# Ending a unit's output products as P6, P3, P7, P7, P3 in other PSUM banks, and rounding the turns on ScalarE: a fused gated linear attention and ELU MLP

## The chip, the core and the metric

The kernel runs on one core of a Trainium2 chip. Five engines share the work: PE (TensorE, matmuls; PEld is its weight load), DVE (VectorE), ACT (ScalarE), POOL (GpSimd) and SP (SyncE, which issues most of the DMAs). The metric is the device time of one execution in microseconds (us); smaller is better.

## What is computed

```
for t in range(S):                       # q, k, v, a_re, a_im: B=4, H=8, S=768, D=48
    new_re = ar * S_re - ai * S_im       # a scaled to a magnitude of at most 0.999
    new_im = ar * S_im + ai * S_re
    S_re, S_im = new_re + k_t v_t^T, new_im
    y[t] = q_t @ S_re
x = y as (B*S, H*D)                      # 3072 tokens x 384
h = x @ w_in                             # 384 x 2048, float64 in memory
g = where(h > 0, h, exp(min(h, 0)) - 1)  # ELU
out = g @ w_out                          # 2048 x 384, float64 in memory
```

## The kernel before

The 3072 tokens are worked off in 12 units, u = 0 to 11, of two batches times 128 tokens. For each unit the attention part gives x, the first MLP product gives h, ELU gives g, and the second product gives the rows of the output. The recurrence is solved in chunks: decays are summed up within a chunk by matmuls (`turned` at L847 for the phases), gates are made from exponentials and sines, and a state `S` is carried from unit to unit.

Units 0 and 1 run plainly while the weights arrive and `convert` turns their float64 words into float32 on DVE. From unit 3 on, h comes from 20 smaller products per unit (`mult`, L1505, eight matmuls each), whose sums are put together by DVE and ACT: `joint` (L1521) adds two of them, `low` (L1526 and L1527, ACT) makes the exponential of ELU, `whole_of` (L1530, DVE) finishes a block of g. `mixed` and `mixed_rest` (L1465, L1485) make the sums of x from which those products start.

From unit 2 on, the second product is also made of seven smaller ones, P1 to P7, each in two halves h = 0 and 1 of eight matmuls (`product`, L1369). Some take sums of blocks of g, which `folded` (L1347, DVE) makes. The results lie in three PSUM tiles of two places each, named (bank, place) here: the tile of bank 0 holds P1, P2 and P3 one after the other at place 0 and P6 at place 1; that of bank 1 holds P5 at place 0 and P7 at place 1; that of bank 2 holds P4. At P6's end DVE adds P6 to a copy of P1 (L1381, into `u2`) and P5 to that (L1382, into `u4`). P7's, P2's and P3's ends (`done`, L1394) write the output rows: three DVE operations for P7, one for P3, a copy on ACT for P2.

`turned` takes the turns of the phase from PSUM, rounds them to a whole number on DVE by adding and subtracting a large constant (L852), and subtracts that from the turns, again on DVE (L855). `waves` then takes sines of it on ACT (L983 to L987), behind a load of ACT's table. `decayed`, `slopes` and `used` are the exponentials of the decays (L914, L930). `scaled` (L1002 for q on DVE, L992 for k on POOL) and `gated` (L1013, q on DVE and k on POOL) make the operands that PE transposes (L1033). `state_sums` (L1089 on DVE, with L1091 on POOL between two of them) adds up the new state; `seam` (L1240) hands x over by DMA; L1260 are the plain MLP products of the units 0 to 2.

Each engine works through its instructions strictly in the order in which the program emits them, and waits at semaphores for other engines. That order is set by hand. For the start and the units 0 to 2 there is a list, `first`. All behind it comes from `plan`: each step is put at a planned time inside its unit, plus a number from the table `SHIFT` (with `@u`, for unit u alone), and the steps are emitted in the order of these times. In the units 10 and 11 the last products run as P6, P6, P3, P7, P7, P3 (each name one half), in the others as P6, P6, P7, P7, P3, P3.

Of the kernel before, what the change touches and what calls it, by code (L numbers as in the profile page):

```python
# [13 lines left out]
ALU = mybir.AluOpType  # L14
# [491 lines left out]
def kernel(  # L506
# [63 lines left out]
    ln_eps = value(float(np.log(2 * EPS)), "ln_eps")  # L570
    quarter = value(float(np.pi / 2), "quarter")
# [270 lines left out]
    def turned(u, n):  # L842
        x = nat[u]
        if n == 0:
# [7 lines left out]
        nc.vector.tensor_scalar(  # L852
            out=z, in0=t, scalar1=MAGIC, scalar2=MAGIC, op0=ALU.add, op1=ALU.subtract
        )
        nc.vector.tensor_tensor(out=z, in0=t, in1=z, op=ALU.subtract)  # L855
# [389 lines left out]
    def hidden(u, f):  # L1245
        inner(u, f)
        elu(u, f)
# [101 lines left out]
    def product(u, k, h):  # L1349
# [3 lines left out]
            1: (0, 0, True), 2: (0, 0, False), 6: (0, 1, False), 5: (1, 0, True),  # L1353
            7: (1, 1, False), 3: (0, 0, True), 4: (2, 0, True),
# [25 lines left out]
        if k == 6:  # L1380
            nc.vector.tensor_tensor(out=u2, in0=to, in1=u2, op=ALU.add)  # L1381
            nc.vector.tensor_tensor(out=u4, in0=x["p", 1][:, 0], in1=u2, op=ALU.add)  # L1382
            return
# [219 lines left out]
    def warm(n):  # L1603
# [23 lines left out]
        "transposed('q', 1)@5": -0.2, "used()": 0.5, "waves()": 0.8, "waves()@3": -3.0,  # L1627
        "whole_of('00', '00')@11": -0.1, "whole_of('00', '00')@3": 0.8,
        "whole_of('10', '10')@4": 0.2, "whole_of('11', 'w')": 0.05, "whole_of('11', 'w')@3": 0.05,
        "whole_of('21', '21')": 0.05, "whole_of('21', '21')@3": 0.05, "whole_of('21', '21')@4": 0.3,  # L1630
        "whole_of('21', '21')@5": 0.1,
# [27 lines left out]
    def gates_of(u, *at):  # L1659
# [8 lines left out]
        (squared, "ai", 1), (joined, 0, 1), (joined, 0, 0), (logarithms, 0, 1), (logarithms, 0, 0),  # L1668
        (ratios, 0, 0), (lengths, 0, 1), (lengths, 0, 0), (sums, 1), (powers, 0, 1), (powers, 0, 0),
        (sums, 0), (warm, 2), (ratios, 0, 1), *2 * [(convert,)], (table, "trig_and_small", 0),  # L1670
# [3 lines left out]
        (scaled, 0, "k", 0), (begun, 1), (ends, 0), (table, "natural_log_exp_and_others", 0),  # L1674
        (scaled, 0, "q", 0), (warm, 2), (warm, 1), (gated, 0, 0), (warm, 1), (scaled, 0, "q", 1),
        (scaled, 0, "k", 1), (warm, 1), (squares, 1), (transposed, 0, "q", 0), (gated, 0, 1),
        (warm, 1), (transposed, 0, "k", 0), (convert,), (joined, 1), (transposed, 0, "q", 1),
        (convert,), (scores, 0, 0), *2 * [(convert,)], (load_qk, 1), (logarithms, 1), (powers, 1),
        (transposed, 0, "k", 1), (lengths, 1), (states, 0, 0), (convert,), (ratios, 1), (warm, 2),
        (slopes, 1), (noted, 1), (values, 0, 0), (convert,), (decays, 1), (warm, 2), (scores, 0, 1),  # L1680
        (states, 0, 1), (angles, 1), (load_v, 1), (warm, 2), (values, 0, 1), (seam, 0), (noted, 0),
        (carry_on, 0), (fetch, "in", 3), (convert,), (scaled, 1), (warm, 2), (ends, 1),
# [44 lines left out]
    def layer_of(u, at_h, at_p):  # L1727
# [33 lines left out]
        if u > NU - 3:  # L1761
            ks[-4:] = (3, 0), (7, 0), (7, 1), (3, 1)
# [105 lines left out]
```

## Time and profile before

| | |
|---|---|
| median of three runs | 648.45 us (648.39, 648.45, 649.2) |
| the profiled execution | 648.65 us, of which the span is 646.9 |
| PE busy | 632.3 us, 98% of the span |
| DVE, ACT, POOL busy | 506.3, 416.8, 168.2 us |
| granted TensorE clock | 0.99 of full speed over the span |

The span is what the profiler sees from the first instruction to the last. A row of the timeline reads: start in us, duration in us, engine, line, operation, output and inputs with their shapes, how many alike were put together, and in brackets how long the engine stood idle before and what released it. A unit is 49 us long in the middle of the run; the first unit's MLP products begin at 44.84 us, and the last matmul ends at 640.7.

### The profile page before, as it was taken

How to read it: one execution, taken by the hardware profiler on the slowest of the kernel's cores; microseconds unless marked ns; L12 is line 12 of the kernel's file. 1: busy time of each engine (PE TensorE's matmuls, PEld its weight loads, DVE VectorE, ACT ScalarE, POOL GpSimd, SP SyncE). 2: the span in 40 equal slices, each digit the busy share in tenths (PEclk: the TensorE clock that was granted, in tenths of full speed). 3: DMA queues.
4: the chain of work that ended last, by engine and by line, in shares of the span. 5: the costliest groups of instructions: out<-in, count | busy, mean ns of one | idle time of the engine just before them, and what ended most of it. 6: DMA issues, size and time to landing. Idle time of an engine off the chain costs nothing.

```text
span 646.9 us, 17126 instructions
## 1 busy us (share of the span) xinstructions
PE 632.3 (98%) x7236; PEld 577.6 (89%) x7236; DVE 506.3 (78%) x801; ACT 416.8 (64%) x684; POOL 168.2 (26%) x200
## 2 busy tenths in 40 slices
PE   8999999999999999999999999999999999999995
PEld 5878886677899999999999999999998999999995
DVE  6999999969689798689589589589679678675481
ACT  5985573765867767776776776766775776661350
POOL 2010100113125415414514513613613603502000
PEclk9889999999999999999999999999999999999999
DMA  9988559435600824424335334344343342112100
GB/s 164 175 138 142 132 164 197 113 67 79 94 9 16 141 51 96 103 57 96 87 61 108 75 70 108 73 76 97 75 84 86 73 97 63 39 31 62 35 2 30
DMA packets 150705, 56.10 MB, mean 87 GB/s; under 512 B 128948, under 2 KB 142428, under 8 KB 150620
## 3 DMA queue, kind: packets, MB, share of 16 engines
q1 hardware_dynamic: 146880, 53.57, 41.3%
q0 software_dynamic: 3520, 1.20, 1.6%
q8 instruction: 59, 0.97, 0.6%
q14 instruction: 26, 0.21, 0.1%
q10 hardware_dynamic: 220, 0.14, 0.1%
HBM read 48.91 MB, written 4.80 MB: 83 GB/s over the span
## 4 chain that ended last, share of the span: by engine, by line
PE 91%; SPq 4%; DVE 2%; DMA 1%; issue 1%; ACT 1%; DVEq 0%; ACTq 0%
PE mlp L1369 29%; PE mlp L1505 16%; PE mlp L1260 10%; PE y L1505 8%; PE w L1033 6%; PE w L1074 4%; PE y L1285 3%; PE mlp L1285 3%; PE y L1119 3%; PE y L1189 3%; PE w L847 2%; PE y L1110 2%; SPq L654 2%; SPq L603 1%; DMA w<-in_moe_w_in_dram 1%; PE w L899 1%
## 5 line engine op out<-in xcount | busy, mean ns | idle before, releaser
L1369 PE MATMUL mlp<-w_out,g 128*128 128x192 f32 x640 | 111.8, 328 | 1.0 <-DVE ee L1381 1.0
L1369 PEld LDWEIGHTS mlp<-w_out,g 128*128 128x128 f32 x640 | 104.2, 190 | 4.4 <-DVE ee L1381 1.6
L1091 POOL TENSOR_TENSOR S<-S,T 128x384 f32<-128x384 f32 x36 | 32.4, 899 | 198.1 <-DVE S L1089 198.1
L1260 PE MATMUL mlp<-x,w_in 128*128 128x256 f32 x288 | 64.0, 381 | 0.0
L1521 DVE TENSOR_TENSOR g<-g,mlp 128x512 f32<-128x512 f32 x45 | 30.9, 686 | 42.2 <-ACT qt L1034 25.3
L1260 PEld LDWEIGHTS mlp<-x,w_in 128*128 128x128 f32 x288 | 54.6, 191 | 7.8
L1347 DVE TENSOR_TENSOR g<-g 128x512 f32<-128x512 f32 x80 | 54.4, 702 | 4.6 <-PE mlp L1369 3.6
L1505 PE MATMUL mlp<-x,w_in 128*128 128x128 f32 x424 | 56.1, 276 | 0.0
L1369 PE MATMUL mlp<-w,g 128*128 128x192 f32 x320 | 54.5, 329 | 0.0
L1240 POOL DMA_DIRECT2D x<-y x62 | 30.7, 502 | 85.8 <-ACT y L1136 54.2
L1369 PEld LDWEIGHTS mlp<-w,g 128*128 128x128 f32 x320 | 51.8, 190 | 0.6
L1526 ACT ACTIVATE ee<-g 128x512 f32<-128x512 f32 x63 | 39.5, 626 | 19.7 <-DVE g L1521 18.5
L1505 PEld LDWEIGHTS mlp<-x,w_in 128*128 128x128 f32 x424 | 51.6, 192 | 0.1
L1530 DVE SCALAR_TENSOR_TENSOR g<-ee,g 128x512 f32<-128x512 f32 x63 | 43.9, 697 | 5.8 <-ACT ee L1527 5.5
L1527 ACT ACTIVATE ee<-ee 128x512 f32<-128x512 f32 x72 | 45.4, 631 | 2.3
L1518 ACT COPY g<-mlp 128x512 f32<-128x512 f32 x36 | 20.9, 582 | 36.0 <-PE mlp L1505 36.0
L1227 ACT COPY x<-y 128x384 f32<-128x384 f32 x20 | 8.6, 482 | 38.1 <-PE y L1119 38.1
L1034 ACT COPY qt<-w 128x512 f32<-128x512 f32 x48 | 25.6, 592 | 11.3 <-PE w L1033 11.3
L914 ACT ACTIVATE n<-w 64x384 f32<-64x384 f32 (+1 forms) x60 | 28.1, 486 | 4.8 <-PE w L899 4.0
L1250 ACT ACT_TABLE_LOAD x24 | 30.8, 1283 | 0.5
L1089 DVE TENSOR_TENSOR S<-w,S 128x384 f32<-128x384 f32 x38 | 21.1, 555 | 11.5 <-PE w L1074 5.3
L1505 PE MATMUL mlp<-x,g 128*128 128x128 f32 x224 | 29.6, 275 | 0.0
(226 smaller groups left out, 1447.5 us busy)
## 6 DMA issues: line engine op xcount, KB each, us to landing
w<-in_moe_w_out_dram SPq DMA_DIRECT2D x8, 768.0 KB, 4.7
g<-in_moe_w_in_dram SPq DMA_DIRECT2D x24, 256.0 KB, 3.1
g<-in_moe_w_out_dram SPq DMA_DIRECT2D x24, 256.0 KB, 2.6
w<-in_moe_w_in_dram SPq DMA_DIRECT2D x16, 288.0 KB, 4.3
vn<-in_v_dram SPq DMA_DIRECT2D x24, 192.0 KB, 4.5
q<-in_q_dram SPq DMA_DIRECT2D x11, 384.0 KB, 5.5
k<-in_k_dram SPq DMA_DIRECT2D x11, 384.0 KB
out_dram<-o SPq DMA_DIRECT2D x44, 96.0 KB, 2.5
```

The costliest lines, as they stand in the source:

```text
L1033: nc.tensor.transpose(t[:, h], of, ident)
L1091: eng.tensor_tensor(out=new_s, in0=new_s, in1=wide, op=ALU.mult)
L1250: nc.scalar.preload_act_table_set(name)
L1260: nc.tensor.matmul(t[:, e], lhsT=w_in[:, i, ts(f + e, C)], rhs=x["x"][:, i], start=(i == 0), stop=(i == NI - 1),)
L1285: nc.tensor.matmul(x["o", n], lhsT=x["g", f // 8][:, f % 8, ts(n, C)], rhs=w_out[:, f], start=(f == 0), stop=(f == NF - 1),)
L1347: nc.vector.tensor_tensor(out=S_of(u, k, h), in0=a, in1=b, op=op)
L1369: nc.tensor.matmul(to, lhsT=a[:, m], rhs=b[:, m], start=(first and h == 0 and m == 0), stop=False, skip_group_check=True,)
L1505: nc.tensor.matmul(x["c" + c][:, ts(m, C)], lhsT=a[:, m], rhs=x["mix"][p], start=(p == BANKS[c][0] and m == 0), stop=False, skip_group_che ...
L1521: nc.vector.tensor_tensor(out=part(u, to), in0=part(u, a), in1=part(u, b), op=op)
L1526: nc.scalar.activation(out=e, in_=part(u, of), func=AF.Relu, scale=-1.0)
L1527: nc.scalar.activation(out=e, in_=e, func=AF.Exp, scale=-1.0)
L1530: nc.vector.scalar_tensor_tensor(out=part(u, to), in0=nat[u]["e", to], scalar=-1.0, in1=part(u, of), op0=ALU.add, op1=ALU.max,)
```

## The change

It has four parts.

1. `product` puts P6 beside P5 (bank 1, place 1) and P7 beside P4 (bank 2, place 1). Bank 0 then holds P1, P2 and P3 alone. The subtraction of P4, which was the last operation at P7's end, is done at P6's end instead, as a third DVE operation (new L1384).
2. The order P6, P6, P3, P7, P7, P3 holds in all units from 2 on.
3. `turned` gives its first step to ACT: an Identity with scale -1 and the large constant as bias makes the constant less the turns; one DVE operation then takes the constant off and adds the turns. There are 24 such calls.
4. `SHIFT` has more and other entries, and `first` stands in another order at some places.

The lines after L568 move down by one, those after L1384 by two.

```diff
+    magic = value(MAGIC, "magic")
...
-        nc.vector.tensor_scalar(
-            out=z, in0=t, scalar1=MAGIC, scalar2=MAGIC, op0=ALU.add, op1=ALU.subtract
-        )
-        nc.vector.tensor_tensor(out=z, in0=t, in1=z, op=ALU.subtract)
+        nc.scalar.activation(out=z, in_=t, func=AF.Identity, scale=-1.0, bias=magic)
+        nc.vector.scalar_tensor_tensor(
+            out=z, in0=z, scalar=MAGIC, in1=t, op0=ALU.subtract, op1=ALU.add
+        )
...
-            1: (0, 0, True), 2: (0, 0, False), 6: (0, 1, False), 5: (1, 0, True),
-            7: (1, 1, False), 3: (0, 0, True), 4: (2, 0, True),
+            1: (0, 0, True), 2: (0, 0, False), 3: (0, 0, True), 4: (2, 0, True),
+            7: (2, 1, False), 5: (1, 0, True), 6: (1, 1, False),
...
             nc.vector.tensor_tensor(out=u4, in0=x["p", 1][:, 0], in1=u2, op=ALU.add)
+            nc.vector.tensor_tensor(out=u2, in0=u2, in1=x["p", 2][:, 0], op=ALU.subtract)
...
-            done(1, 0, to, (u2, ALU.add), (x["p", 2][:, 0], ALU.subtract))
+            done(1, 0, to, (u2, ALU.add))
...
-        "state_sums(0, (1,))@3": 1.2, "state_sums(0, (1,))@4": -0.8,
+        "state_sums(0, (1,))@3": 0.4, "state_sums(0, (1,))@4": -0.8, "state_sums(1, (1,))": 0.9,
...
-        (angles, 0, 1), (summed, 0), (convert,), (decayed, 0, 0), (convert,), (turned, 0, 0),
-        (summed, 1), (turned, 0, 1), (warm, 1), (decayed, 0, 1), (waves, 0, 0), (waves, 0, 1),
+        (angles, 0, 1), (summed, 0), (warm, 1), (convert,), (decayed, 0, 0), (convert,),
+        (turned, 0, 0), (summed, 1), (turned, 0, 1), (decayed, 0, 1), (waves, 0, 0), (waves, 0, 1),
...
-        (states, 0, 1), (angles, 1), (load_v, 1), (warm, 2), (values, 0, 1), (seam, 0), (noted, 0),
-        (carry_on, 0), (fetch, "in", 3), (convert,), (scaled, 1), (warm, 2), (ends, 1),
-        (table, "trig_and_small", 1), (convert,), (turns, 1), (warm, 1), *3 * [(convert,)],
+        (scores, 0, 1), (load_v, 1), (states, 0, 1), (angles, 1), *2 * [(warm, 2)], (scaled, 1),
+        (noted, 0), (values, 0, 1), (carry_on, 0), (fetch, "in", 3), (convert,), (ends, 1),
+        (convert,), (table, "trig_and_small", 1), (convert,), (seam, 0), (convert,), (warm, 1),
+        (turns, 1), (convert,), (waves, 1), (inner, 0, 2), (inner, 0, 0), (fetch, "in", 4),
...
         ks = [(k, h) for k in (1, 4, 2, 5, 6, 7, 3) for h in range(2)]
-        if u > NU - 3:
-            ks[-4:] = (3, 0), (7, 0), (7, 1), (3, 1)
+        ks[-4:] = (3, 0), (7, 0), (7, 1), (3, 1)
```

PE at the end of unit 7's output products, before. The first two rows are P5, into the tile of bank 1, the next two P6, into that of bank 0; each tile is called `mlp` with its number, and `g` with a number is a block of ELU's output or a sum of such blocks.

```order
L1369 MATMUL mlp_4866<-w64_1445,g_4408 128x192 x4
L1369 MATMUL mlp_4866<-w64_1445,g_4409 128x192 x4
L1369 MATMUL mlp_4606<-w64_1446,g_4408 128x192 x4
L1369 MATMUL mlp_4606<-w64_1446,g_4409 128x192 x4
L847 MATMUL w_4905<-n_4872,sum_turns_110 128x384
L847 MATMUL w_4909<-n_4872,sum_turns_110 128x384
L1369 MATMUL mlp_4866<-w_out_59,g_1444 128x192 x8
L1369 MATMUL mlp_4606<-w_out_59,g_4408 128x192 x4
L1369 MATMUL mlp_4606<-w_out_59,g_4409 128x192 x4
L1505 MATMUL mlp_4963<-x_4854,g_1443 128x128 x4
```

The same place after the change:

```order
L1370 MATMUL mlp_4867<-w64_1447,g_4410 128x192 x4
L1370 MATMUL mlp_4867<-w64_1447,g_4411 128x192 x4
L1370 MATMUL mlp_4867<-w64_1448,g_4410 128x192 x4
L1370 MATMUL mlp_4867<-w64_1448,g_4411 128x192 x4
L848 MATMUL w_4908<-n_4873,sum_turns_112 128x384
L848 MATMUL w_4912<-n_4873,sum_turns_112 128x384
L1370 MATMUL mlp_4608<-w_out_59,g_4410 128x192 x4
L1370 MATMUL mlp_4748<-w_out_59,g_1446 128x192 x8
L1370 MATMUL mlp_4608<-w_out_59,g_4411 128x192 x4
L1507 MATMUL mlp_4965<-x_4855,g_1445 128x128 x4
```

P3's first half (bank 0) now stands ahead of P7, P7 has gone from the tile of bank 1 to that of bank 2, and P6 from that of bank 0 to that of bank 1. In the units 10 and 11, which had this order already, only the tiles differ.

DVE in unit 8, beside the first output products, before. `S` is the state, `a` the masked scores, `g<-ee,mlp` the block `whole_of(11, w)` of ELU's output.

```order
L1089 TENSOR_TENSOR S<-w,S 128x384
L1197 TENSOR_TENSOR a<-y_5173,mask 128x512
L1197 TENSOR_TENSOR a<-y_5174,mask 128x512
L1089 TENSOR_TENSOR S<-w,S 128x384 x2
L1530 SCALAR_TENSOR_TENSOR g<-ee,mlp 128x4x128
L690 TENSOR_REDUCE seen<-g 128x1
L1530 SCALAR_TENSOR_TENSOR g<-ee,g 128x4x128
```

And after:

```order
L1090 TENSOR_TENSOR S<-w,S 128x384
L1198 TENSOR_TENSOR a<-y_5175,mask 128x512
L1198 TENSOR_TENSOR a<-y_5176,mask 128x512
L1090 TENSOR_TENSOR S<-w,S 128x384
L1532 SCALAR_TENSOR_TENSOR g<-ee,mlp 128x4x128
L691 TENSOR_REDUCE seen<-g 128x1
L1532 SCALAR_TENSOR_TENSOR g<-ee,g 128x4x128
L1348 TENSOR_TENSOR g<-g 128x512
L1348 TENSOR_TENSOR g<-g 128x4x128
L1090 TENSOR_TENSOR S<-w,S 128x384
```

The third state sum, `state_sums(1, (1,))`, has moved from ahead of the block to behind two sums of `folded`. It stood ahead in the units 5 to 8.

DVE in the middle of unit 11, the last one, before. `n<-w` and `needs<-n` are the two steps of `pronounced`, which decide whether a slower general path must run behind.

```order
L1521 TENSOR_TENSOR g<-g,y_6485 128x4x128
L1530 SCALAR_TENSOR_TENSOR g<-ee,g 128x4x128
L1559 TENSOR_REDUCE n<-w 1x1
L1560 TENSOR_SCALAR needs<-n 1x1
L1530 SCALAR_TENSOR_TENSOR g<-ee,g 128x4x128
L1521 TENSOR_TENSOR g<-y_6484,g 128x4x128
L1347 TENSOR_TENSOR g<-g 128x512
L1347 TENSOR_TENSOR g<-g 128x4x128
```

And after:

```order
L1523 TENSOR_TENSOR g<-mlp,g 128x4x128
L1523 TENSOR_TENSOR g<-g,y_6487 128x4x128
L1532 SCALAR_TENSOR_TENSOR g<-ee,g 128x4x128
L1523 TENSOR_TENSOR g<-y_6486,g 128x4x128
L1532 SCALAR_TENSOR_TENSOR g<-ee,g 128x4x128
L1348 TENSOR_TENSOR g<-g 128x512
L1348 TENSOR_TENSOR g<-g 128x4x128
L1532 SCALAR_TENSOR_TENSOR g<-ee,g 128x4x128
L1523 TENSOR_TENSOR g<-g,mlp 128x4x128
```

The two steps of `pronounced` have gone from here to among the sums of the second half's `folded`, and a `whole_of` stands one joint later.

More of the change, by code (lines that the diff above doesn't have):

```diff
@@ L1613 @@
     SHIFT = {
[13 rows of a table removed]
[L1627 to L1631, printed above, removed]
[3 rows of a table added]
+        "gated()": 0.05, "gated(None, ('k',))": 0.5, "gated(None, ('k',))@5": -0.2,
+        "gated(None, ('q',))": 0.45, "gated(None, ('q',))@11": -0.2, "hidden(0,)": 0.05,
[27 rows of a table added]
     }
@@ L1724 @@
-        (summed_in, 6), (elu, 2, 10), (summed_in, 8), (joined, 4), (summed_in, 7), (elu, 2, 8),
-        (combined, 3, 1), (inner, 2, 12), (transposed, 3, "k", 1),
+        (angles, 0, 1), (summed, 0), (warm, 1), (convert,), (decayed, 0, 0), (convert,),
+        (turned, 0, 0), (summed, 1), (turned, 0, 1), (decayed, 0, 1), (waves, 0, 0), (waves, 0, 1),
+        (begun, 1), (ends, 0), (table, "natural_log_exp_and_others", 0), (scaled, 0, "q", 0),
+        (warm, 2), (warm, 1), (scaled, 0, "k", 0), (gated, 0, 0), (scaled, 0, "q", 1),
@@ new lines @@
+        *2 * [(convert,)], (elu, 0, 12), (convert,), (elu, 1, 10), *4 * [(convert,)], (load_qk, 2),
+        (convert,), (fetch, "out", 6), (project, 1, 0, 0, 4), (convert,), (inner, 1, 14),
+        (slopes, 2), *3 * [(convert,)], (project, 1, 1, 0, 4), (project, 0, 0, 0, 4), (angles, 2),
+        (lengths, 2), (fetch, "out", 7), (convert,), (project, 0, 0, 4, 8), (elu, 1, 14),
+        (project, 0, 1, 0, 4), (decays, 2), (convert,), (project, 1, 0, 4, 8), (carried, 2),
+        (convert,), (table, "trig_and_small", 2), *2 * [(convert,)], (turns, 2), (waves, 2),
@@ new lines @@
+        (scaled, 2), (convert,), (table, "natural_log_exp_and_others", 2), (project, 0, 1, 4, 8),
+        (convert,), (begun, 3), (convert,), (table, "trig_and_small", 3), (project, 0, 1, 8, 12),
+        (convert,), (project, 1, 1, 4, 8), (squares, 3), (gated, 2), (project, 1, 0, 8, 12),
+        *2 * [(convert,)], (joined, 3), (convert,), (transposed, 2, "k", 1),
+        (transposed, 2, "q", 1), (convert,), (table, "natural_log_exp_and_others", 3), (convert,),
+        (ends, 2), (convert,), (logarithms, 3), (powers, 3), (project, 1, 1, 8, 12), (load_qk, 3),
@@ new lines @@
+        (combined, 4, 0), (inner, 2, 4), (inner, 2, 6), (ends, 3), (load_a, 4), (inner, 2, 2),
+        (summed_in, 4), (load_v, 3), (inner, 2, 0), (elu, 2, 4), (scaled, 3), (elu, 2, 6),
+        (summed_in, 3), (elu, 2, 2), (waves, 3), (gated, 3, None, ("k",)), (elu, 2, 0),
+        (gated, 3, None, ("q",)), (project, 0, 0, 12, 16), (inner, 2, 10), (transposed, 3, "k", 0),
+        (warm, 2), (begun, 4), (folded, 2, 0, (3, 1)), (load_v, 4), (inner, 2, 8), (squares, 4),
+        (elu, 2, 10), (load_qk, 4), (transposed, 3, "q", 0), (transposed, 3, "q", 1),
```

81 lines of the change are left out of this document (31 added, 50 removed), and 42 rows, old and new, of the table SHIFT.

## The prediction

> **What bounds the kernel now.** I read the busy times first, then the chain of work that ended last, then what PE waits for, and last the timeline around those waits.
>
> ```profile
> span 646.9 us, 17126 instructions
> PE 632.3 (98%) x7236; PEld 577.6 (89%) x7236; DVE 506.3 (78%) x801; ACT 416.8 (64%) x684; POOL 168.2 (26%) x200
> PE 91%; SPq 4%; DVE 2%; DMA 1%; issue 1%; ACT 1%; DVEq 0%; ACTq 0%
> ```
>
> PE is the bound: 98% busy, 91% of the chain. It issues the same matmuls after the change, so whatever is won is a gap in PE's row that closes, and the whole stake is 646.9 - 632.3 = 14.6 us, most of it in the first 66 us. How long a unit takes is read from two products that stand once in each, in the chain:
>
> ```profile
> 259.34 3.62 PE mlp L1505 x32
> 286.22 6.70 PE mlp L1369 x40
> 308.46 3.62 PE mlp L1505 x32
> 335.34 6.91 PE mlp L1369 x40
> 357.80 3.62 PE mlp L1505 x32
> ```
>
> Unit 4 goes from 259.34 to 308.46, 49.12 us; unit 5 to 357.80, 49.34. The 0.22 between them is in the first output products, 6.70 against 6.91: something there is late in one unit and not in the other. The list of waits names it, with the other place where PE waits for DVE (columns: us, times, longest):
>
> ```profile
> PE mlp L1369 <- DVE ee L1381: 1.0, 2, 0.5
> ...
> PEld mlp L1369 <- DVE g L1530: 1.1, 5, 0.2
> ```
>
> Five times 0.2 us on a block of g, and twice 0.5 us on L1381, the sum at P6's end. Both are what this change touches.
>
> **The third state sum (SHIFT).** Unit 8, where the block is made:
>
> ```profile
> 483.38 0.56 DVE L1089 TENSOR_TENSOR S<-w,S 128x384 f32<-128x384 f32 x1 [0.37 <-PE w L1074]
> 484.02 0.83 POOL L1091 TENSOR_TENSOR S<-S,T 128x384 f32<-128x384 f32 x1 [1.55 <-DVE S L1089]
> 484.88 0.56 DVE L1089 TENSOR_TENSOR S<-w,S 128x384 f32<-128x384 f32 x1 [0.94 <-PE mlp L1369]
> 485.36 0.68 DVE L1530 SCALAR_TENSOR_TENSOR g<-ee,mlp 128x512 f32<-128x512 f32 x1
> 486.09 1.27 PEld L1369 LDWEIGHTS mlp<-wt,g 128*128 128x128 f32 x8 [0.22 <-DVE g L1530]
> ```
>
> DVE stands 0.94 us at the third state sum. The row blames a matmul, but POOL's product of S ends at 484.85 and the sum starts at 484.88: it waits for POOL. Behind it is queued the block (485.36), behind that PE's weight load, 0.22 us late. With the sum moved behind two sums of `folded`, the block can start at about 483.94, some 1.4 us earlier, and the 0.22 goes. The moved sum costs DVE 0.56 wherever it is; nobody reads the state before the next unit's products with it, tens of us on. The `folded` sums come about 0.9 us earlier, so nothing is late next. Four units have that order (5 to 8): 4 x 0.21 = **-0.84 us**. The fifth wait is in unit 11, below.
>
> **Banks, and the order of the last products.** Units 10 and 11, where DVE's sums stand between P6 and P3:
>
> ```profile
> 596.71 0.36 DVE L1381 TENSOR_TENSOR ee<-mlp,ee 128x192 f32<-128x192 f32 x1 [4.25 <-PE mlp L1369]
> 597.11 0.36 DVE L1382 TENSOR_TENSOR ee<-mlp,ee 128x192 f32<-128x192 f32 x1
> 597.12 5.47 PE L1369 MATMUL mlp<-w_out,g 128*128 128x192 f32 x32 [0.52 <-DVE ee L1381]
> ...
> 635.22 5.47 PE L1369 MATMUL mlp<-w_out,g 128*128 128x192 f32 x32 [0.52 <-DVE ee L1381]
> ```
>
> P6 ends at e = 596.60, L1381 reads its bank until 597.07, and P3, which writes the same bank, starts at 597.12. After the change P3's bank is read by nobody, so it starts at e, and 0.52 is won. P7, 8 matmuls later, now writes the bank from which the new third operation reads P4. Three operations at a pitch of 0.40 (596.71 to 597.11) from e + 0.11 end at e + 1.27; a half of P3 lasts 5.47 / 4 = 1.37, of which I subtract a little since P7's weights must be loaded ahead: P7 waits 0 to 0.3, which leaves -1.04 to -0.44 for the two units. I take 0.17, in the middle: **-0.35 us** for each, **-0.70** in all. In the other units P7 used to stand between P6 and P3, so nothing waited and nothing is won; with P3's half and two turns ahead of it, P7 comes 2.8 us behind P6, twice what the three operations need. P7's end has one operation less, P6's one more: DVE's sum is the same. The Trainium skill, PSUM — Partial Sum Buffer, section "PSUM bank collisions raise a hardware error", says that two engines must be kept apart by bank and not by address; the row at 597.12, where a write to place 0 waits for a read of place 1, agrees. By that rule P7's new place beside P4 is a wait that the edit brings in; without it the two units would give -1.04, with it -0.70.
>
> **The last unit.** Unit 11 has two more gaps, and DVE does other work ahead of them:
>
> ```profile
> 619.74 0.14 DVE L1560 TENSOR_SCALAR needs<-n 1x1 int32<-1x1 f32 x1
> ...
> 622.52 0.69 DVE L1530 SCALAR_TENSOR_TENSOR g<-ee,g 128x512 f32<-128x512 f32 x1
> 623.12 0.68 DVE L1521 TENSOR_TENSOR g<-g,mlp 128x512 f32<-128x512 f32 x1
> ...
> 623.86 3.04 PE L1369 MATMUL mlp<-wt,g 128*128 128x192 f32 x16 [0.31 <-DVE g L1521]
> 625.33 1.27 PEld L1369 LDWEIGHTS mlp<-wt,g 128*128 128x128 f32 x8 [0.20 <-DVE g L1530]
> ```
>
> From the steps of `pronounced` on (619.74) DVE works without a pause to the joint that PE waits for (623.12). The two steps take about 0.48 us of it (the operations around them come 0.6 apart elsewhere, 622.52 to 623.12, and 1.08 here) and are moved behind. So the joint, and the `whole_of` from which the block's exponential on ACT is released, come 0.48 or more earlier, enough for 0.31 and for 0.20: **-0.51 us**. Behind the last product DVE has the same operation to do as before, so the end loses nothing.
>
> **The rounding on ACT.** The two operations before, and the nearest to the new one:
>
> ```profile
> L852 DVE TENSOR_SCALAR n<-w 128x384 f32<-128x384 f32 x24 | 13.2, 549 | 1.9 <-PE w L847 1.9
> L855 DVE TENSOR_TENSOR n<-w,n 128x384 f32<-128x384 f32 x24 | 13.4, 558 | 0.8
> L914 ACT ACTIVATE n<-w 128x384 f32<-128x384 f32 x20 | 8.7, 488 | 4.1 <-PE w L899 4.0
> ```
>
> DVE loses 24 x 0.549 = 13.2 us, ACT gets 24 x 0.488 = 11.7. Neither bounds the kernel (78% and 64%), so from unit 2 on this is worth nothing in itself; the cover is PE's row, and it is thin where these lines stand:
>
> ```profile
> 452.80 2.04 DVE L1002 TENSOR_TENSOR q<-q,n 128x768 f32<-128x768 f32 x1
> 457.48 0.42 DVE L1485 TENSOR_TENSOR pair<-x 128x256 f32<-128x256 f32 x1
> 458.09 1.06 PE L1505 MATMUL mlp<-x,w_in 128*128 128x128 f32 x8
> 461.71 0.49 PE L1033 MATMUL w<-ident,qg 128*128 128x128 f32 x3
> ```
>
> ACT does the exponentials of `used` first and ends them by my count at 450.8; the two Identities end at 451.8, the two DVE steps at 452.5, and `scaled` starts at about 452.46 instead of 452.80. Then come `mixed` (2.1 us), now ahead of P7's end, and that end at 456.6 to 457.25. The third product of the next unit (458.09) takes the place in PSUM that P7's end reads: a margin of 0.84. `gated` ends at 459.0, and the transposes want it at 461.71. Cost: 0, with the margin as the point where it turns.
>
> **The start.** Here ACT is the tight engine, and two Identities more in each of the first two units' chains do count.
>
> ```profile
> 15.99 1.64 ACT L930 ACTIVATE n<-mlp 128x384 f32<-128x384 f32 x4
> 20.22 0.96 DVE L1013 TENSOR_TENSOR qg<-q,cs 128x768 f32<-128x768 f32 x1
> 21.32 1.94 PE L1033 MATMUL w<-ident,qg 128*128 128x128 f32 x8 [0.59 <-DVE qg L1013]
> 39.24 1.50 ACTq L1240 DMA_DIRECT2D x<-y  x2
> 44.84 5.47 PE L1260 MATMUL mlp<-x,w_in 128*128 128x256 f32 x24
> 60.07 0.66 PE L1033 MATMUL w<-ident,kg 128*128 128x128 f32 x4 [0.73 <-ACT kt L1034]
> 66.12 4.15 PE L1260 MATMUL mlp<-x,w_in 128*128 128x256 f32 x18
> ```
>
> The Identities stand between the exponentials at 15.99, so the sines and the first gated q (20.22) come 0.93 later, two Identities of 0.488 less a little, and the first transposes (21.32) too. Following each engine's new order, ACT has made this good by 38 us. The hand-over of x at 39.24 now stands behind two steps of `noted`, the copies and a table load, at about 43; it comes late enough to hold the first MLP product (44.84) by 0 to 1.1 us. Behind it DVE has less to do and is 0.7 to 1.2 ahead, the 0.73 at 60.07 should go, and the products at 66.12, from which on PE hardly stands still, start between 65.2 and 67.2 by this walk. I take 65.8: **-0.3 us**, with the ends -0.9 and +1.1.
>
> The clock can change this by more than the walk. Two windows (columns: us, PE busy, count, granted clock, DMA share, GB/s):
>
> ```profile
> 22.00:23.00 1.00, 1.00 (x6) 0.50 1.00 148
> ...
> 42.00:43.00 1.00, 1.00 (x2) 0.50 0.94 279
> ```
>
> PE runs at half its clock in these and in the microseconds beside them, some 3 us each time, and ahead of each lies a stretch in which PE waited for the gates or for x. A third such window could take up to half of its length, 1.5 us; one that falls away gives as much. The Trainium skill, TensorE: Matmul & The Clock Gate, section "What's actually happening" in Part 1, has the gate step down after an idle window of about 3.4 us, and the windows run freely: the two slow stretches behind waits agree. By it a later gate or hand-over can bring a third one, for which its 3.4 give an estimate of 1.7 us at most.
>
> **The sum.** -0.84 - 0.70 - 0.51 - 0.3 = -2.35 us. From the profiled execution's 648.65 (its span of 646.9 and 1.75 around it) that is 646.3; it lay 0.2 above the median of 648.45, so against that **646.1 us**. A difference of 0.2%, 1.3 us, is about what a measurement of this kernel tells from none: faster means under 647.15, slower over 649.75.
>
> **Rivals.**
>
> *The start gets longer.* For it: ACT has 0.98 us more ahead of the first gate and x goes late. Against it: DVE is ahead there. It costs +1.1 instead of -0.3, so 647.5: no difference. Chance 0.16.
>
> *The stalls only change places.* P7 waits for L1384 as long as P3 did for L1381, and the joint in unit 11 is held by ACT: then just -0.84 and -0.3 are left, 647.3. Against it speaks that P7 has 1.37 us of P3 ahead, 0.10 more than the three operations need. Chance 0.11.
>
> *Slower: PE waits in every unit at the third product.* `mixed`, and behind it P7's end, now follow ACT's Identities. If ACT's exponentials end over 0.84 us later than I counted, P7's end passes 458.09, and PE stands in all of the nine units from 3 on. At 1.25 us late it is 0.4 in each, 9 x 0.4 = 3.6, less 2.35 won: +1.3, or 649.7; from there it decides. At 1.6 late it is 9 x 0.76 = 6.8 and 652.9. For it: before, P7's end was ahead of `mixed`; against: ACT's table load is earlier. Chance 0.14.
>
> *More is won at the start.* If the hand-over comes in such a way that the slow window at 42 falls away (1.3 of the 1.5) and the start also reaches its near end (0.6 more), 644.2. Chance 0.14.
>
> **Chances and range.** My own case has 0.45, within 645.2 to 647.1 (the ends of the start and of P7's wait). Faster: 0.45 + 0.14 and the near edge of the first two rivals, 0.02: 0.61. Within 0.2%: 0.23. Slower: 0.14 and the far edge of the longer start, 0.02: 0.16. The range leaves out most of the slower case and the last half of the gain at the start: 644.2 to 649.0.
>
> **What would show it.** The units 4 to 8 all at 49.1 us; no wait of PE on L1530 and none on L1382, but one of 0.1 to 0.3 on L1384 in units 10 and 11; PE's products of 66.12 at 65.2 to 66.1. I am wrong if PE waits on L1396, or if a third window at 0.50 stands in the first 60 us.

## The result, and the profile after

The changed kernel takes 644.47 us (644.26 to 644.8, four runs) against 648.83 for the kernel before (648.39 to 649.7): ratio 0.9932, interval 0.9914 to 0.9949, faster by 4.4 us. Forecast were 646.1 and a range of 644.2 to 649.0: the sign held and the time lies at the near end of the range, with nearly twice the gain that I had summed. A later set of runs of the same two kernels gave 644.41 and 648.8.

The head of the page and of its chain, after:

```profile
span 642.8 us, 17116 instructions
PE 628.7 (98%) x7236; PEld 576.0 (90%) x7236; DVE 489.3 (76%) x777; ACT 428.5 (67%) x707; POOL 159.0 (25%) x201
PE 95%; ACT 2%; DVE 1%; issue 1%; POOL 0%; DVEq 0%; ACTq 0%; POOLq 0%
```

PE is still the bound with the same 7236 matmuls. Its busy time fell by 3.6 us all the same. At half clock the same matmuls count as busy for twice as long (the turns below, 2.93 and 1.46 us), but one such stretch of 3.4 us less explains at most half of the 3.6; the rest was not followed. DVE lost 17 us and ACT gained 12; neither bounds the kernel.

The chain, the two rows that stand once in a unit:

```profile
257.41 3.62 PE mlp L1507 x32
284.29 6.70 PE mlp L1370 x40
306.54 3.62 PE mlp L1507 x32
333.42 6.70 PE mlp L1370 x40
355.66 3.62 PE mlp L1507 x32
```

Units 4 and 5 last 49.13 and 49.12 (306.54 - 257.41, 355.66 - 306.54), and 6.91 has become 6.70. The list of waits has lost PE's rows on DVE's L1381 and on the joint; of the waits of the output products' weight loads for DVE this is left:

```profile
PEld mlp L1370 <- DVE ee L1384: 0.6, 2, 0.3
...
PEld mlp L1370 <- DVE g L1532: 0.2, 1, 0.2
```

The tail (timeline, PE and DVE):

```profile
593.64 5.63 PE L1370 MATMUL mlp<-w_out,g 128*128 128x192 f32 x32
...
594.69 0.35 DVE L1384 TENSOR_TENSOR ee<-ee,mlp 128x192 f32<-128x192 f32 x1
...
620.06 3.04 PE L1370 MATMUL mlp<-wt,g 128*128 128x192 f32 x16
...
630.74 5.63 PE L1370 MATMUL mlp<-w_out,g 128*128 128x192 f32 x32
```

P3 and P7 follow P6 at once, and their 32 matmuls last 5.63. Where P7 waits for nothing, the same 32 take 5.36 (last experiment), so its wait for the third sum is 0.27. And the start:

```profile
42.42 1.46 PE L848 MATMUL w<-n,sum_turns 128*128 128x384 f32 x4
43.71 5.34 PE L1261 MATMUL mlp<-x,w_in 128*128 128x256 f32 x24
...
57.71 1.04 PE L1034 MATMUL w<-ident,kg 128*128 128x128 f32 x8
...
62.98 0.31 PE L1075 MATMUL w<-vn,kg 64*64 64x48 f32 x2 [1.02 <-issue]
...
64.43 7.82 PE L1261 MATMUL mlp<-x,w_in 128*128 128x256 f32 x35
```

The turns of unit 1 took 2.93 us before, at half clock; here they take 1.46. The wait of 0.73 on ACT ahead of the last transposes is gone, and a wait for nothing that the profile shows, 0.73 before, is 1.02 here. The products that began at 66.12 begin at 64.43.

By stage, in the two profiles (before less after): the start 1.69; unit 3 0.33 (49.41 to 49.08); units 5 to 8 0.21 each, 0.84; unit 9 0.04; unit 10 0.52 (47.82 to 47.30); unit 11 1.0. The plain products between 66 us and unit 3 lost 0.09, and the wrap-up behind the last matmul about 0.2. That gives the 4.1 us between the spans.

### The profile page after: what moved, and what is told of

It reads as the page before. It is cut to its first block, busy times and chain, and to the rows that moved or that the text cites. A ratio compares the mean times of both kernels' runs of the same rounds, so it can differ in the third digit from the quotient of the medians.

```text
span 642.8 us, 17116 instructions
## 1 busy us (share of the span) xinstructions
PE 628.7 (98%) x7236; PEld 576.0 (90%) x7236; DVE 489.3 (76%) x777; ACT 428.5 (67%) x707; POOL 159.0 (25%) x201
## 4 chain that ended last, share of the span: by engine, by line
PE 95%; ACT 2%; DVE 1%; issue 1%; POOL 0%; DVEq 0%; ACTq 0%; POOLq 0%
PE mlp L1370 29%; PE mlp L1507 16%; PE mlp L1261 10%; PE y L1507 9%; PE w L1034 6%; PE w L1075 4%; PE y L1286 3%; PE mlp L1286 3%; PE y L1120 3%; PE y L1190 3%; PE w L848 2%; PE y L1111 2%; PE mlp L1609 1%; PE w L900 1%; PE w L1042 1%
## 5 line engine op out<-in xcount | busy, mean ns | idle before, releaser
L1092 POOL TENSOR_TENSOR S<-S,T 128x384 f32<-128x384 f32 x36 | 34.0, 946 | 204.9 <-DVE S L1090 204.9
L1529 ACT ACTIVATE ee<-ee 128x512 f32<-128x512 f32 x72 | 45.4, 631 | 2.3
L1507 PE MATMUL y<-x,w_in 128*128 128x128 f32 x216 | 28.6, 275 | 0.0
```

Of the source, the lines that this page charges most:

```text
L1092: eng.tensor_tensor(out=new_s, in0=new_s, in1=wide, op=ALU.mult)
L1507: nc.tensor.matmul(x["c" + c][:, ts(m, C)], lhsT=a[:, m], rhs=x["mix"][p], start=(p == BANKS[c][0] and m == 0), stop=False, skip_group_che ...
L1529: nc.scalar.activation(out=e, in_=e, func=AF.Exp, scale=-1.0)
```

## Experiments

Two questions were open: where the start's 1.7 us came from (0.3 was forecast), and which part of the change carries which piece. For the start there were two theories. ORDER: the list and what it puts on ACT and DVE. GATE: PE's clock, which falls to half in windows that lie differently against the work in each kernel and run. Beside the time I give the start of the first MLP product and of the long row of products (44.84 and 66.12 before, 43.71 and 64.43 after), and unit lengths. The runs of the kernel before went from 646.6 to 650.6 in these studies.

The mean granted clock of a run tells about how many half-clock stretches it had: the first profile of before has 0.994 and two of them (at 21 and at 41.7 us), that of after 0.996 and one (at 20 us).

**The kernel before once more.**

> The kernel before, unchanged, for a second profile of its start. What is open is why the first MLP product begins at 43.71 us after the change and at 44.84 before. Theory GATE: in the profile of before PE ran at half clock from 41.7 to 45.1 us, and the windows of the gate lie where they happen to lie against the kernel's start; then this profile shows the second slow stretch shifted by some tenths, or none at all, and where there is none the product begins by 43.6. Theory ORDER (rival): the new order of the start is what counts; then this profile repeats 44.84 within 0.2 and the slow stretch at 41.7.

Its time was 649.53 us; first product 44.36, long row 66.27. The half clock (from 40.8 to 44.2 by the windows' clocks) came 0.9 earlier than in the first profile. So the window moves against the work, as GATE says; but PE waited 1.51 instead of 0.73 for "issue" (no releaser that the profile shows) at 64 us, and the long row began where it had. What the earlier first product gave, another stall took.

**Old list, the rest new.** Edit on the kernel after: the whole list of before, which orders everything up to unit 4's first steps and differs in most of its lines; the pieces around the two turns are

```diff
-        (turned, 0, 0), (summed, 1), (turned, 0, 1), (decayed, 0, 1), (waves, 0, 0), (waves, 0, 1),
+        (summed, 1), (turned, 0, 1), (warm, 1), (decayed, 0, 1), (waves, 0, 0), (waves, 0, 1),
...
-        (convert,), (table, "trig_and_small", 1), (convert,), (seam, 0), (convert,), (warm, 1),
+        (states, 0, 1), (angles, 1), (load_v, 1), (warm, 2), (values, 0, 1), (seam, 0), (noted, 0),
```

> The kernel after with the start's list of before; banks, order of the products, rounding on ACT and the table of shifts stay as after. ORDER: the start's gain of 1.7 us goes, and ACT's two Identities make it later than before as well: the products that began at 66.12 before and 64.43 after begin at 66.0 to 67.2, time about 646.2 to 647.2. GATE: where the slow second stretch stays away, they begin at 64.5 to 65.3 and the time is 644.6 to 645.4.

647.36 us (ratio 0.9969, 0.9955 to 0.9983), with runs from 646.3 to 650.0; the profile is of the slowest. In it the window at 40 to 45 is at full clock:

```profile
43.95 5.35 PE L1261 MATMUL mlp<-x,w_in 128*128 128x256 f32 x24
50.87 1.10 PE L1034 MATMUL w<-ident,qg 128*128 128x128 f32 x8 [1.57 <-DVE qg L1014]
...
66.49 0.31 PE L1075 MATMUL w<-vn,kg 64*64 64x48 f32 x3 [1.78 <-issue]
67.97 4.24 PE L1261 MATMUL mlp<-x,w_in 128*128 128x256 f32 x11
```

The first product comes early, and then PE waits 1.57 for a gate on DVE and 1.78 for "issue". The long row begins at 67.97, and the clock falls behind it (0.73 from 66 to 70). Time and long row lie beyond what ORDER expected (647.2 and 67.2): the list is worth some 2 to 3 us once ACT does the rounding. Its units 3 and 4 last 49.08 and 49.13 as after's do, so nearly all of that lies ahead of unit 3.

**Fill in the gap.** Edit on the kernel before, in `ends`:

```diff
+            if u == 1:
+                warm(2)
             t = work([C, NB, C // L, H])
```

> The kernel before with two more warming matmuls of unit 1 in the 0.6 us in which PE waits at 40.8 to 41.4 us for DVE's copy; nothing else is moved. GATE: the window that ends at 41.7 is no longer idle enough, PE stays at full clock, the turns take 1.46 instead of 2.93 us, the first MLP product begins 1.0 to 1.4 earlier (43.4 to 43.8), and the time falls by 0.5 to 1.3 to about 647.4. ORDER: no difference, 648.4 to 648.9.

648.19 us against 649.31 (ratio 0.9991, 0.9981 to 1.0001). Timeline and a window with its clock:

```profile
40.97 1.56 PE L847 MATMUL w<-n,sum_turns 128*128 128x384 f32 x4
...
63.81 0.33 PE L1076 MATMUL w<-vn,kg 64*64 64x48 f32 x7 [1.62 <-issue]
...
42.00:43.00 1.00, 1.00 (x6) 1.00 1.06 183
```

No half clock, the turns in 1.56, the first product at 42.59, 2.2 earlier than in the first profile of before, as GATE expects. Yet the long row began at 65.36, only 0.8 earlier, since PE then waited 0.49 on a gate and 1.62 for "issue". The time is not told apart from before's. One profile does not show that the fill kept the clock up, either: the run with the steps of `pronounced` moved, below, has before's start without this fill, and no half clock there.

**Fill taken away.** Edit on the kernel after:

```diff
-        (scores, 0, 1), (load_v, 1), (states, 0, 1), (angles, 1), *2 * [(warm, 2)], (scaled, 1),
+        (scores, 0, 1), (load_v, 1), (states, 0, 1), (angles, 1), (scaled, 1),
```

> The kernel after without the four warming matmuls that stand ahead of unit 1's scaling (1.48 us of PE at 37.3 us); nothing else is moved. GATE: the window of 37.2 to 40.6 becomes idle enough, PE falls to half clock at about 40.6, the turns take 2.9 instead of 1.46, and the time rises by 0.5 to 1.5 to about 645.5. ORDER: the matmuls are only fill, and the time stays at 644.2 to 644.8.

647.8 us, runs from 646.0 to 653.7. Two windows at half clock follow one another:

```profile
42.35 0.60 PE L964 MATMUL w<-once,pair 48*128 48x32 f32 x2 [1.41 <-DVE once L962]
43.47 2.77 PE L848 MATMUL w<-n,sum_turns 128*128 128x384 f32 x4
46.03 6.72 PE L1261 MATMUL mlp<-x,w_in 128*128 128x256 f32 x24
...
42.00:43.00 1.00, 0.65 (x3) 0.50 0.20 52
...
46.00:48.00 2.00, 2.00 (x6) 0.50 1.06 164
```

Four matmuls whose result nobody reads cost about 3 us when they are left out (the ratio goes from 0.9932 to 0.9983). The mean clock of the ten runs is 0.988 to 0.994, in the runs of after 0.992 to 0.996. So the fill counts, as GATE says, and for more than I had allowed. The profile is of the slowest run and shows stalls too (1.41 here, 2.13 for "issue" at 66 us), so not all of the 3 us need be the clock. The Trainium skill, TensorE: Matmul & The Clock Gate, Part 1, section "What's actually happening", has the gate's windows last about 3.4 us and run freely. The traces agree: in the profiles seen the half clock lasts 3.4 or twice that (41.7 to 45.1, 40.8 to 44.2, 42.0 to 48.8), and the stretch near 42 us, where there is one, begins anywhere from 40.7 to 42.7.

**The kernel after once more.**

> The kernel after, unchanged, beside the kernel before on this chip, and for a second profile of its start. GATE: PE stays at full clock from 40 to 45 us here too, the first MLP product begins at 43.7 within 0.2, the products of 64.43 within 0.5, and the runs lie closer together (about 0.5 us apart) than those of the kernel before (1.6). If instead the slow stretch had been absent by luck, this profile may show one at 41 to 45, and the runs spread as before's do. The gain over before: 4.0 to 4.8 us.

644.41 us (ratio 0.9937, 0.9918 to 0.9955), full clock from 40 to 45, first product 43.77, long row 63.66 with no stall of 1 us ahead of it. The runs do spread, though, from 643.2 to 645.4, and two of six have a mean clock of 0.992. So how much is the gate in all? Of before's 70 runs in these studies 17 had a mean clock of 0.995 or more, median 648.15 (a run at 0.994 can still have the slow stretch at 42, as the first profile shows). Of after's ten runs six had, median 644.41. At like clock the change gains 3.7, then; the 0.7 that is left of the medians' 4.4 would come from fewer slow stretches. That the change itself makes them fewer is not shown: of the ten runs with only `pronounced` moved, whose start is before's, eight had 0.995 or more.

**New list alone.** Edit on the kernel before: the list of after, the diff of the second study with its signs turned round.

> The kernel before with the start's list of after alone; rounding on DVE, banks, order of the products and shifts as before. By the steps of the prediction (a walk of the order) the list without the two Identities should win more than 0.3: by ORDER the products of 66.12 begin at 64.0 to 65.0 and the time is 1.1 to 2.1 below before, and all of the later units keep before's lengths (49.12 and 49.34). By GATE it depends on whether the window at 40 to 45 stays at full clock: then 64.0 to 64.5, otherwise 65.5 to 66.5 and the time within 0.5 of before.

648.12 us against 648.8 (ratio 0.9989, 0.9968 to 1.001: unclear), runs from 645.9 to 651.3. First product 44.09, long row 65.65, at half clock from 42.0 to 45.4. By itself the list wins 0.5 in the profile, with the half clock in both.

**Rounding on ACT alone.** Edit on the kernel before:

```diff
-        nc.vector.tensor_scalar(
-            out=z, in0=t, scalar1=MAGIC, scalar2=MAGIC, op0=ALU.add, op1=ALU.subtract
-        )
-        nc.vector.tensor_tensor(out=z, in0=t, in1=z, op=ALU.subtract)
+        nc.scalar.activation(out=z, in_=t, func=AF.Identity, scale=-1.0, bias=magic)
+        nc.vector.scalar_tensor_tensor(
+            out=z, in0=z, scalar=MAGIC, in1=t, op0=ALU.subtract, op1=ALU.add
+        )
```

> The kernel before with the rounding on ACT alone (list, banks, order, shifts as before). From unit 2 on both theories expect no difference, as long as P7's end and the gates are covered: units of 49.1 and 49.3 us as before. The rival that the prediction held for slower expects PE to wait at the third product of each unit, 0.4 or more, and units of 49.5 or more. At the start ACT is the tight engine: the first gate is 0.9 later, the products of 66.12 begin at 66.5 to 67.5, and the time rises by 0.4 to 1.4.

650.81 us: slower, ratio 1.0036 (1.0021 to 1.0052). First product 45.45 and long row 66.49, 0.4 later than before; the rest is not at the start. The list of waits and the timeline name one place:

```profile
PE mlp L1506 <- DVE o L1395: 0.6, 1, 0.6
...
210.78 1.16 PE L1506 MATMUL mlp<-x,g 128*128 128x128 f32 x8 [0.60 <-DVE o L1395]
```

That is unit 3's first product, waiting for P7's end of unit 2. It is the rival that I had held for slower, once, and not in each unit: at the third product of the units 4 to 9 P7's end is still 2.72 ahead, as in before. From the long row to unit 3 the profile is 0.65 longer than before's. Units 3 and 4 lasted 49.57 and 49.62 instead of 49.41 and 49.13; unit 4's 0.49 lies in its state products, with no wait that the profile names, and units 5 to 8 were as before. Start, wait and the two units make 1.67, all of the difference between the two profiled executions (650.32 and 648.65).

**Rounding back on DVE.** Edit on the kernel after: the same lines with their signs turned round.

> The kernel after with the rounding back on DVE (list, banks, order, shifts as after). If the move to ACT is worth nothing in itself, the units stay at 49.13 us and the end as after; the start's first gate comes up to 0.9 earlier, which shifts the work against the gate's windows: 643.5 to 645.0 by ORDER, or up to 646.5 by GATE where the slow window at 41 to 45 comes back. If the move is what makes room on DVE, single units grow by 0.2 to 0.6 (PE waiting for L1384 or for the gates), and the time is 646 to 649.

646.16 us (ratio 0.9965, 0.9948 to 0.9982), 1.7 above after. The profile is of the slowest run, 649.65: half clock from 42.7 to 46.1 and again between 66 and 70, long row 66.42. But the clock does not make the 1.7: the seven runs with a mean of 0.995 or more have a median of 646.27, 1.9 above after's. In the profile unit 4, whose third product waits for P7's end, lasts 49.87 instead of 49.13, and unit 5 49.64:

```profile
PE mlp L1507 <- DVE o L1396: 0.3, 1, 0.3
```

So the move to ACT costs about 2 us in the old plan and is wanted in the new one. That the plan's shifts fit the one or the other is the likely reason; no run shows it.

**Banks and order alone.** Edit on the kernel before: of the change's diff the lines of `product` and `ks`, that is

```diff
-            1: (0, 0, True), 2: (0, 0, False), 6: (0, 1, False), 5: (1, 0, True),
-            7: (1, 1, False), 3: (0, 0, True), 4: (2, 0, True),
+            1: (0, 0, True), 2: (0, 0, False), 3: (0, 0, True), 4: (2, 0, True),
+            7: (2, 1, False), 5: (1, 0, True), 6: (1, 1, False),
...
-        if u > NU - 3:
-            ks[-4:] = (3, 0), (7, 0), (7, 1), (3, 1)
+        ks[-4:] = (3, 0), (7, 0), (7, 1), (3, 1)
```

and P4's subtraction at P6's end.

> The kernel before with the new banks, the third sum at P6's end and the order P6, P3, P7, P7, P3 in all units; list, rounding and shifts as before. By the prediction's step: in units 10 and 11 P3 no longer waits, P7 waits 0.16 for the third sum, both shorter by 0.35 (by the trace of after: by 0.5, 47.82 to 47.3 for unit 10), units 3 to 9 unchanged at 49.1 and 49.3, and 0.7 to 1.1 us in all: by time 0 to 1.5 below before, the start's scatter being larger. The rival (the stalls only change places) expects unit 10 at 47.7 to 47.8.

658.14 us: slower by 9, ratio 1.0133 (1.0114 to 1.0152). I had expected a gain. Units 3 to 9 went to 50.2 to 51.4, and unit 10 from 47.82 to 47.80 only. The gain is there all the same: P3 follows P5 and P6 at once in both of the last units,

```profile
639.99 5.36 PE L1369 MATMUL mlp<-w,g 128*128 128x192 f32 x32
645.19 5.63 PE L1369 MATMUL mlp<-w_out,g 128*128 128x192 f32 x32
```

and the stretch from P5 to the end of P3 is 0.52 shorter in unit 10 and 0.53 in unit 11, as in the kernel after. In unit 10 a wait at its third product takes it away again. The waits, then DVE and PE at the end of unit 4's products:

```profile
PE mlp L1506 <- DVE o L1395: 7.8, 9, 1.5
...
312.69 0.42 DVE L1486 TENSOR_TENSOR pair<-x 128x256 f32<-128x256 f32 x1
313.03 1.75 DVE L1013 TENSOR_TENSOR qg<-q,cs 128x1536 f32<-128x1536 f32 x1
314.70 0.61 DVE L1395 TENSOR_TENSOR o<-mlp,ee 128x192 f32<-128x192 f32 x2
...
315.37 1.16 PE L1506 MATMUL mlp<-x,w_in 128*128 128x128 f32 x8 [0.97 <-DVE o L1395]
```

P7 comes half a P3 later, so the plan puts its end behind `gated` on DVE (1.75 us), and the third product of the next unit waits for it in all of the units 3 to 10: 1.52 in unit 3 (and 0.20 at a later product there), 0.97 in each of the units 4 to 9, 0.28 in unit 10. In the kernel after, `SHIFT` has "gated(None, ('q',))" at 0.45 instead of 0.05, and the order is turned round (timeline of after, unit 7):

```profile
449.55 1.05 ACT L853 ACTIVATE n<-w,magic 128x384 f32<-128x384 f32 x2
...
451.11 1.19 DVE L1003 TENSOR_TENSOR q<-q,n 128x768 f32<-128x768 f32 x1
...
454.35 0.61 DVE L1396 TENSOR_TENSOR o<-mlp,ee 128x192 f32<-128x192 f32 x2
454.88 1.75 DVE L1014 TENSOR_TENSOR qg<-q,cs 128x1536 f32<-128x1536 f32 x1
...
455.54 1.06 PE L1507 MATMUL mlp<-x,w_in 128*128 128x128 f32 x8
```

P7's end is done at 454.96, 0.58 ahead of the product; I had counted 0.84. At the other boundaries from unit 3 on it is 0.35 (into unit 4) to 2.27 ahead. That `SHIFT` is what takes the 9 us back was not run alone, but little else is left: with the old list (above) each unit is within 0.3 us of after's, and with the rounding on DVE the units 3 to 9 together are 1.45 us longer.

**The third state sum alone.** Edit on the kernel before:

```diff
-        "state_sums(1, (1,))@4": 2.0, "state_sums(1, (1,))@5": 0.2, "summed_in(10,)": -0.3,
+        "state_sums(1, (1,))": 0.9, "state_sums(1, (1,))@4": 2.0, "state_sums(1, (1,))@5": 0.2, "summed_in(10,)": -0.3,
```

> The kernel before with one more entry in the table of shifts, the third state sum 0.9 later. By the prediction's step: the units 5 to 8 go from 49.34 to 49.13 each, 0.84 in all, nothing else moves. Rival: the moved sum stands in front of a sum that PE waits for, and the units stay at 49.3 or grow.

648.2 us (ratio 0.999, 0.9978 to 1.0003: not told apart by time). The profile shows it: units 6, 7 and 8 are at 49.13, 49.12 and 49.13, and the waits on the block are gone; unit 5 is at 49.29, 0.16 of it without a named wait. Unit 8:

```profile
482.77 0.56 DVE L1089 TENSOR_TENSOR S<-w,S 128x384 f32<-128x384 f32 x1 [0.37 <-PE w L1074]
483.24 0.68 DVE L1530 SCALAR_TENSOR_TENSOR g<-ee,mlp 128x512 f32<-128x512 f32 x1
483.41 0.83 POOL L1091 TENSOR_TENSOR S<-S,T 128x384 f32<-128x384 f32 x1 [1.55 <-DVE S L1089]
...
486.22 0.55 DVE L1089 TENSOR_TENSOR S<-w,S 128x384 f32<-128x384 f32 x1
```

The block now runs beside POOL's product, and the third sum begins 3 us after the block.

**The steps of `pronounced` alone.** Edit on the kernel before:

```diff
-        "low('31', '31')": -0.05, "low('31', '31')@11": 0.05, "noted()": -1.2, "pronounced()": -0.2,
+        "low('31', '31')": -0.05, "low('31', '31')@11": 0.05, "noted()": -1.2, "pronounced()": 2.8,
```

> The kernel before with the shift of pronounced from -0.2 to 2.8 alone. By the prediction's step: in unit 11 PE's waits of 0.31 and 0.20 on DVE ahead of the P4 products go, and the stretch from the first output product of unit 11 (620.78) to the product that waited (623.86) shrinks from 3.08 by 0.3 to 0.5. Rival: the joint is held by the exponentials on ACT or by the other whole_of, and the stretch stays at 3.08 or loses less than 0.1.

648.23 us (ratio 0.9986, 0.9976 to 0.9996). The stretch from 619.03 to 622.11 stayed at 3.08: the rival was right.

```profile
618.24 0.69 DVE L1530 SCALAR_TENSOR_TENSOR g<-ee,g 128x512 f32<-128x512 f32 x1 [0.40 <-ACT ee L1527]
...
622.11 3.04 PE L1369 MATMUL mlp<-wt,g 128*128 128x192 f32 x16 [0.32 <-DVE g L1521]
```

Where the two steps stood DVE now waits 0.40 for an exponential on ACT. They had filled a gap that was there anyway. What wins at this place in the kernel after is the order of joints and blocks: there a joint stands ahead of this block, DVE works through, and the stretch is 2.61 (617.45 to 620.06). No run has that order alone.

The 0.9 us between the medians are not from here: unit 11 is as long as before's (38.26 from its first product to the end of its last). At a mean clock of 0.995 or more the runs' median is 648.03, before's 648.15. So an edit that moves nothing on PE can show 0.9 us, with an interval clear of 1, by the clock alone. And the profile shows what before's start does without the half clock at 42:

```profile
41.16 1.56 PE L847 MATMUL w<-n,sum_turns 128*128 128x384 f32 x4
42.77 5.35 PE L1260 MATMUL mlp<-x,w_in 128*128 128x256 f32 x24
...
63.16 0.32 PE L1074 MATMUL w<-vn,kg 64*64 64x48 f32 x3 [0.70 <-issue]
64.60 1.56 PE L1260 MATMUL mlp<-x,w_in 128*128 128x256 f32 x6
```

The first product begins 0.94 earlier than in the kernel after, and the long row at 64.60, 1.5 us earlier than in the first profile of before and only 0.17 behind after's.

**A version on top.** Edit on the kernel after:

```diff
+            if u == 1:
+                warm(1)
...
-        ks[-4:] = (3, 0), (7, 0), (7, 1), (3, 1)
+        if u != NU - 2:
+            ks[-4:] = (3, 0), (7, 0), (7, 1), (3, 1)
+        else:
+            ks[-4:] = (3, 0), (3, 1), (7, 0), (7, 1)
```

> The kernel after with two small additions: one warming matmul of unit 1 in the 0.37 us in which PE waits for DVE's copy at 41.4, and the order P6, P3, P3, P7, P7 in unit 10 alone, so that P7 does not wait for the third sum. Unit 10 should go from 47.3 to 47.1. GATE: the runs with a mean clock under 0.993 (2 of 10 so far for after) become rarer, the median is 0.2 to 0.5 below after's, 643.9 to 644.3. Rival: the extra matmul delays the turns by 0.2 and the first products with them, and the time is that of after or 0.2 above.

643.75 us against 649.12 (ratio 0.9916, 0.9902 to 0.993). Unit 10 went from 47.30 to 47.03; its last 32 products take 5.36 instead of 5.63, so P7 no longer waits:

```profile
594.51 5.36 PE L1372 MATMUL mlp<-w_out,g 128*128 128x192 f32 x32
```

Its own profile, of the slowest run, had half clock from 42.2 to 45.6 in spite of the warming matmul (long row 64.72), and the intervals of its ratio and of after's overlap, so only the 0.27 of unit 10 is shown.

## Why the prediction was right or wrong

The time lies inside the range because the terms for the units came, and most of what was won beyond the sum, over a microsecond, came at the start. Part of that was luck: the first profile of before had the slow stretch at 42 us and that of after had not.

- **State sum, -0.84:** right to 0.01, cause and size, and shown alone in three of its four units.
- **P3 and P7 in the units 10 and 11, -0.35 each:** the step was right, and shown alone in both units by the run with banks and order; both of its sizes were too small. P7's wait was 0.27 (0.17 forecast), and P3's start was held by 0.68, not by the 0.52 in the row. In unit 10 before, the row of P5 and P6 began at 591.24 and P3 at 597.12, 5.88 later; without a stall the same distance is 5.20 (625.54 to 630.74 in unit 11 after). Rows overlap by 0.16, so an idle time in brackets shows too little. The row behind the stall also lasted 5.47 instead of 5.36, another 0.11. Net 0.68 + 0.11 - 0.27, -0.52 and -0.53.
- **Unit 11's other gaps, -0.51:** -0.47 came, for another reason. My step that the two steps of `pronounced` hold the joint failed; ACT's exponential stood behind them. And the 0.20 of the weight load stayed, with nothing lost by it, since PE's 16 matmuls take 2.88 there in both kernels; all of the 0.47 is the wait that shows as 0.31, with 0.16 of overlap again. That the size came so close is luck.
- **Banks and order in the other units, 0:** the sum came out, the reasoning was too short. "Nothing waited" was misread, for before's list of waits has eight weight loads that wait 0.2 for L1382; they are gone after, and as unit 4 lasts 49.13 in both kernels nothing was lost by them. More weighs that the edit costs 9 us in the old plan. The prediction had the mechanism as its slower rival (P7's end later than the third product, PE waiting in nine units), but laid it to ACT's Identities; what pushes P7's end is P7's own move.
- **Rounding on ACT, 0:** right for the units in their new plan, with a margin that is nearly used up in places (0.35 into unit 4). In unit 7 luck helped: ACT's exponentials ended 1.27 us later than I had counted, more than the 0.84 at which the slower rival was to begin. P7's end came in time since `scaled` took 1.19 us, not the 2.04 that I had taken over from before.
- **The start, -0.3:** the term was mis-sized. The profiles show -1.69 and -2.46 (66.12 to 63.66), but against before's start without the half clock at 42 (64.60) the same two show only -0.17 and -0.94. From the runs at like clock, 3.7 less the 2.4 that the profiles have behind the start, I estimate 1.3. One reason is a step: the hand-over of x was to come at about 43 and hold the first product by 0 to 1.1, and it came at 40.66 and held nothing. At full clock the first product even begins 0.94 later than in before (43.71 and 42.77); what wins it back lies behind, where a wait of 0.50 for a gate and that of 0.73 on ACT are gone. The rival "more is won at the start" had named the slow stretch and a nearer end of the start; I had given it 0.14. I had also taken one profile's start as the start, and it moves by 2 us from run to run (64.60 to 66.65 in five profiles with before's list, fill and rounding).
- **Unit 3, 0.33:** not forecast, and its cause not shown. In seven profiles with before's tiles and order unit 3 lasts 49.23 to 49.64, in six with the new ones and new shifts 49.08 to 49.52, so part or all of it may be scatter.

What stays open: how the start's gain splits between the list and the rounding. Each kernel with one of them drew other windows and other "issue" stalls (0.3 to 2.1 us), so single profiles can't divide it.

## What to carry to other kernels

In a kernel whose bound engine is 98% busy, a change of buffers or order has to be costed together with the plan around it: the same edit cost 9 us in the old plan and won 0.5 us in each of two units in the new one, because of one operation that went behind another on a neighbouring engine. Read a stall from start to start of the rows around it, not from the idle time in brackets. Before laying a wait to what stands ahead of it on its engine, ask what that engine would wait for if those instructions were gone. And where the clock moves a run by more than the gain in question, compare runs of like mean clock before giving a difference a cause.

## What the hardware showed

The clock's slow windows do not lie fixed against the kernel: in two profiles of the kernel before the second one began at 41.7 and 40.8, and with only the end of the kernel changed it was absent once. Fill that only keeps PE busy moves the odds (no run of ten at 0.995 or more with four matmuls taken out of the kernel after, six of ten with them), but no single profile is decided by it: one with a matmul added had the slow window, one with before's start and nothing added had none.

The prediction had the clock step down behind an idle window, and PE was not idle. In the 3.4 us ahead of the step at 41.7 the profile of before counts it busy for 2.80 us, with the new list alone 3.03 us ahead of the step at 42.0, and in the last experiment all of the 3.4 us ahead of that at 42.2. In each of them some 1.5 us or more went to the 32 matmuls of L956 or L957, two columns wide; whether such matmuls count for less was not tried.

PE stands for 0.3 to 2.1 us at its state products around 64 us in nearly every profile, waiting for nothing that the profile shows; the same kernel had 0.73 and 1.51 there, another 1.02 and none listed. The place goes with the count of instructions ahead of it: in the profiles that have it, it comes behind the 61st of 64 small matmuls with the old list, behind the 62nd with the new one, behind the 57th with two fill matmuls (four rows) added, and only in the next group with four taken out. What it is, no run told.

The same product of `scaled` on DVE (128x768) lasts 0.95 to 2.04 us. It is long where POOL's product of k (1.81 us) runs beside it: in unit 7 before, POOL ends at 454.02 and DVE at 454.84; in unit 7 after, at 451.47 and 452.30.
